# Spreading the 64-token output products of a fused attention and gated-MLP kernel over twelve slots, with their words made at slot heads

## The chip, the core and the metric

The kernel runs on one core of a Trainium2 chip. The metric is the device time of one execution in microseconds (us); lower is better. The engines are TensorE (PE, its weight loads are PEld), VectorE (DVE), ScalarE (ACT), GpSimd (POOL) and SyncE (SP), which issues most DMAs. Each engine takes its instructions in the order in which the program lists them for it.

## The reference

```python
def sm_attn(qq, kk, vv):              # softmax(scale * qq kk^T) vv, per batch and head
    ...
p_packed = sm_attn(p, k, v)           # 32 packing queries per head
x = sm_attn(q, p_packed, p_packed)    # (8 batches, 8 heads, 576 tokens, 64)
x = x.transpose(0, 2, 1, 3).reshape(4608, 512)
g, val = x @ w_gate, x @ w_val        # 512 -> 1536
out = (silu(g) * val) @ w_out         # 1536 -> 512, float32
```

## The kernel before

**Words.** Every float32 operand of a large product is split into a high word (a cast to fp32r, on ACT) and a low word (source minus high, on DVE, line 1194 in `low`). A product is then three matmuls: low by high, high by low, high by high.

**Batches and slots.** Batches 0 and 1 run first in other code. Batches 2 to 7 run in `batch2`, in twelve slots each, one for each chunk of 128 columns of the 1536 (`fc`, 0 to 11). A slot makes the gate and value products of one chunk (`gv_half`, line 1306): 12 matmuls of 256 columns for its first half, 12 of 320 columns for its second. ACT takes the SiLU (line 1315), DVE multiplies (`hmul2`, line 1324) into an h tile. Between these lie the calls of `fill`, which place the attention work of later batches by a table of slot and place (`run`), and in odd slots the 16 matmuls that make the next pair's weights (`m_part`, line 296).

**Output products.** For the 512 tokens of a batch that fill whole tiles of 128, `products` (line 1241) runs seven slots behind: 12 matmuls of 256 columns in the first half of a slot (`which` 0, on the words `ho`) and 9 in the second half (`which` 1, on `hs`). They add up over the six pairs of chunks of one half batch in four PSUM banks, `acc[0]` to `acc[3]`. Of `acc[1]` only the first 256 columns are used. At the sixth pair ACT and DVE take the banks out (`first_results`, `results`, line 1271).

**The 64-token products.** A batch has 576 tokens, so 64 are left over. Those of batches 2g and 2g+1 share one tile of 128 rows, `t4` (one small tile for each pair k of chunks), so there are four groups g of six pairs. `p4_step(k, b)` (line 1279) makes the words of pair k (one ACT cast, line 1285, one DVE subtraction, line 1194, both into `t_parts`, which holds two pairs; `t_first` in group 0) and at once issues the pair's six matmuls of 512 columns (`out_mm`, line 739). Where it is called sets what waits:

- group 0: in batch 2, slots 1 to 5, one pair a slot and two in slot 5. Batch 2 has no `products` before slot 7, so these slots are light.
- groups 1 and 2: all six pairs in one slot, slot 2 of batches 4 and 6 (`tail`), at the places 2 to 7 of `fill`.
- group 3: after the last slot, one pair in each of five rounds of the epilogue loop, between the two halves of `products`, and the sixth pair at the very end, through `end_out`, which also writes it out.

**PSUM.** Four banks hold `acc`. Four more are a ring that `gv_half`, `m_part` and the attention products take in turn (`ring_ps`); the sums of groups 1 to 3 take a ring bank too.

Of the kernel before, what the change touches and what calls it, by code (L numbers as in the profile page):

```python
# [25 lines left out]
P = 128  # L26
# [110 lines left out]
def tile_pack_attention_swiglu(ctx: ExitStack, tc: tile.TileContext, qT, q0, kT, v, vq, pT, wgv, wout, out):  # L137
# [547 lines left out]
    t4 = {}  # L685

    def t4_at(b, fc):
        k = fc // 2
        d = t4.setdefault(b // 2, {})
        if k not in d:  # L690
            d[k] = pool.tile([P, 2, P], F32, tag="t4", bufs=NFC // 2 + 1, name="t4")
        return d[k][:, fc % 2]
# [13 lines left out]
    def gv_chunk(b, fc, is_b, fill, behind, between):  # L706
        odd = b % 2
        n = NB if is_b else NA
        off = (0 if odd else 256) if is_b else (320 if odd else 0)
        mh, ml = ms[b, fc // 2]  # L710
        ah, al = a2[b]
        f = fc % 2
        pgs = []
        for s in range(2):
            pg = ring_ps("gv")
            pgs.append(pg)
            i = 0
# [11 lines left out]
        hf = early.tile([P, 256], F32, tag="hf", bufs=2, name="hf")  # L729
        o, o4 = (64, 0) if is_b and odd else (0, 256)  # L730
        nc.vector.tensor_tensor(hf, pgs[1][:, o : o + 256], sg[:, o : o + 256], op=ALU.mult)
        if is_b:
            r, r4 = slice(64 * odd, 64 * odd + 64), slice(o4, o4 + 64)
            nc.vector.tensor_tensor(t4_at(b, fc)[:, r], pgs[1][:, r4], sg[:, r4], op=ALU.mult)
        return h_split(hf, nc.scalar, nc.vector, between)
# [84 lines left out]
    with tc.manual_schedule(engines={mybir.EngineType.PE}):  # L820
        warm_ps = ps_aux.tile([P, 512], F32, tag="aux", name="warm_ps")

        ones = early.tile([P, 2 * P], F32, tag="hf", bufs=2, name="ones")
# [11 lines left out]
        with tc.manual_schedule(  # L835
# [135 lines left out]
            def half(i):  # L971
                fc, is_b = order[i]
                if fc // 2 < SPLIT:
                    return h0[fc // 2][:, fc % 2, 256 * is_b : 256 * is_b + 256]
                if i not in hs:
                    hs[i] = [early.tile([P, 256], F32, tag="hf", bufs=2, name="hf")]
                return hs[i][0]
# [7 lines left out]
            def hmul(i):  # L985
# [3 lines left out]
                if is_b:  # L989
                    r = slice(256, NB)  # L990
                    nc.vector.tensor_tensor(t4_at(0, fc)[:, :64], x[:, r], sg[:, r], op=ALU.mult)
# [5 lines left out]
            def h_low(i):  # L997
                hs[i].append(h_tile("hl"))
                nc.vector.tensor_tensor(hs[i][2], hs[i][0], hs[i][1].bitcast(F32), op=ALU.subtract)

# [82 lines left out]
        more = mid.tile([P, 4, 4 * P], F32, name="more")  # L1083
# [5 lines left out]

        def chunk(b, fc, is_b, fill, behind):  # L1090
            odd = b % 2
            n = NB if is_b else NA
            off = (0 if odd else 256) if is_b else (320 if odd else 0)
            mh, ml = ms[b, fc // 2]
            ah, al = a2[b]
            pgs = []
            for s in range(2):
                pg = ring_ps("gv")
                pgs.append(pg)
                todo = [(m_, a_, g) for m_, a_ in ((ml, ah), (mh, al), (mh, ah)) for g in range(NPAR)]  # L1100
                for i, (m_, a_, g) in enumerate(todo):
                    nc.tensor.matmul(
                        pg[:, :n], m_[:, g, fc % 2, s * P : (s + 1) * P], a_[:, g, off : off + n],
                        start=(i == 0), stop=(i == 5),
                    )
                fill()
            sg = pool.tile([P, NB], F32, tag="sg", bufs=1, name="sg")
            nc.scalar.activation(sg[:, :n], pgs[0][:, :n], AF.Silu)
            behind()
            at = b, int(is_b), fc // 2  # L1110
            if fc % 2 == 0:
                raw[at] = places.pop(0)
            x = raw[at][:, fc % 2].rearrange("p t n -> p (t n)")
            o, o4 = (64, 0) if is_b and odd else (0, 256)
            nc.vector.tensor_tensor(x, pgs[1][:, o : o + 256], sg[:, o : o + 256], op=ALU.mult)
            if is_b:
                r, r4 = slice(64 * odd, 64 * odd + 64), slice(o4, o4 + 64)
                nc.vector.tensor_tensor(t4_at(b, fc)[:, r], pgs[1][:, r4], sg[:, r4], op=ALU.mult)
# [106 lines left out]
        def products(at, which, fill):  # L1225
# [13 lines left out]
            for n, (bank, col, x, (wh, wl)) in enumerate(todo):  # L1239
                for i, (h_, w_) in enumerate(((lo, wh), (hi, wl), (hi, wh))):  # L1240
                    nc.tensor.matmul(  # L1241
                        acc[bank][:, QC * col : QC * col + QC], h_[:, x], w_,
                        start=(k == 0 and i == 0 and col == 0), stop=(k == 5 and i == 2 and (bank, col) in ((0, 1), (1, 0), (2, 1), (3, 1))),
                    )
                if n in ((1, 3) if which == 0 else (0, 2)):
                    fill()
            if k == 5:
# [12 lines left out]
        def results(b, half):  # L1260
# [16 lines left out]
        p4, t4_t = [], []  # L1277

        def p4_step(k, b):
            if k == 0:  # L1280
                t4_t.append(t4.pop(b // 2))
                p4.append(ps() if b > 1 else ps_acc.tile([P, 512], F32, tag="acc", name="acc4"))
            hh, hl = (t4_parts[:, k % 2, i] for i in range(2))
            src = t4_t[0].pop(k).rearrange("p f t -> p (f t)")
            nc.scalar.copy(hh, src)
            low(hl, src, hh)
            if k == 5 and b == B - 1:
                end_out(p4[0], (b // 2) * 2 * S + 4 * P, (hh, hl))
            else:
                for i in range(2):  # L1290
                    out_mm(p4[0], hh, hl, i * P, 2 * k + i)
            if k == 5:
                if b < B - 1:
                    emit_out(p4[0], (b // 2) * 2 * S + 4 * P, 0)
                p4.clear(), t4_t.clear()
# [22 lines left out]
        def hmul2(b, fc, is_b, pg, sg):  # L1318
# [6 lines left out]
            if is_b:  # L1325
                r, r4 = slice(64 * odd, 64 * odd + 64), slice(o4, o4 + 64)
                nc.vector.tensor_tensor(t4_at(b, fc)[:, r], pg[:, r4], sg[:, r4], op=ALU.mult)

        def batch2(b):
            nonlocal u_t, t4_parts  # L1330
            run = plan_of(b)
            for fc in range(NFC):
                t = (b - 2) * NFC + fc
                cur, nxt = pair_at(t), pair_at(t + 1)
                tail = b % 2 == 0 and fc == 2 and b > 2
                count, step = [0], [0]
# [7 lines left out]
                def fill():  # L1344
# [18 lines left out]
                    if b == 2 and (fc, c) in ((1, 3), (2, 3), (3, 3), (4, 3), (5, 3), (5, 7)):  # L1363
                        p4_step(fc - 1 + c // 7, 1)
# [12 lines left out]
                for is_b in (False, True):  # L1377
                    pg = gv_half(b, fc, is_b, 0)
# [3 lines left out]
                    run(fc, "b" if is_b else "a")  # L1382
                    hmul2(b, fc, is_b, pg, sg)
# [3 lines left out]
                    if is_b:  # L1387
                        run(fc, "hb")
                        if nxt and fc % 2:
# [10 lines left out]
        with tc.manual_schedule(  # L1400
            engines={mybir.EngineType.DVE, mybir.EngineType.Activation, mybir.EngineType.Pool}
        ):
            for b in range(2, B):
                batch2(b)
            for j in range(7):
# [52 lines left out]
```

## Time and profile before

| | |
|---|---|
| median of 3 runs | 744.02 us (742.9 to 746.06) |
| profiled execution: its own time | 745.82 us |
| its span, first to last instruction | 744.0 us |
| PE busy | 707.9 us (95%) |
| DVE busy | 496.5 us (67%) |
| ACT busy | 394.4 us (53%) |
| POOL busy | 173.5 us (23%) |
| mean granted TensorE clock, of full speed | 0.984 |

Times are from the span's start. A timeline row gives the start, the duration, the engine (a q behind it: its sequencer issues), the line, the operation, out<-in, the shape, and how many alike follow each other (x6); a bracket gives the idle time of the engine before it and what ended it. The duration of a matmul is its latency: matmuls overlap, and the rate is the distance between two starts. Where a row holds several, its duration runs from the first start to the last end.

### The profile page before, as it was taken

To read this page: it belongs to the slowest core of one execution; us is meant where nothing else is said; L and a number is where in the kernel's file an instruction comes from. 1 tells how busy PE (TensorE), PEld (TensorE's weight loads), DVE (VectorE), ACT (ScalarE), POOL (GpSimd) and SP (SyncE) were. 2 spreads that over 40 slices of the span, in tenths; PEclk is the share of its full clock that TensorE was granted. 3 is DMA by queue.
4 is the path that set the end of the run, shared out by engine and by line. 5 is a ranking of instruction groups with operands and counts; after the bars stand their busy time and mean duration, and the time that the engine had idled before them with its cause. 6 is when DMAs were issued, how large, how long until landed. Compare 5 with 4: busy or idle time off the path is not lost.

```text
span 744.0 us, 16252 instructions
## 1 busy us (share of the span) xinstructions
PE 707.9 (95%) x6503; PEld 621.6 (84%) x6503; DVE 496.5 (67%) x1093; ACT 394.4 (53%) x714; POOL 173.5 (23%) x349
## 2 busy tenths in 40 slices
PE   7999999999976999999989999999989999999986
PEld 5778788788856798999968989899877998989976
DVE  4986776668643687678754787778862787545453
ACT  3888456536633475636634467546652556343331
POOL 0000001223311433231311313223221232323241
PEclk9999999999998999999989999999999999999999
DMA  9999983021240532434242333452430324210001
GB/s 359 349 348 341 339 344 118 3 71 59 91 150 0 195 126 91 179 129 162 102 146 81 128 128 136 144 189 91 177 143 16 115 87 170 87 57 30 1 29 43
DMA packets 25435, 103.26 MB, mean 139 GB/s; under 512 B 6672, under 2 KB 7952, under 8 KB 16656
## 3 DMA queue, kind: packets, MB, share of 16 engines
q1 hardware_dynamic: 25072, 102.00, 37.1%
q8 instruction: 51, 0.84, 0.4%
q10 hardware_dynamic: 288, 0.23, 0.1%
q14 instruction: 24, 0.20, 0.1%
HBM read 86.44 MB, written 15.78 MB: 137 GB/s over the span
## 4 chain that ended last, share of the span: by engine, by line
PE 90%; DVE 5%; ACT 3%; issue 1%; ACTq 0%; DVEq 0%
PE gv L1306 30%; PE acc L1241 25%; PE acc L739 10%; PE aux L296 6%; PE gv L966 5%; PE aux L739 4%; PE gv L720 4%; PE gv_aux L296 1%; PE gv_aux L520 1%; PE gv_aux L436 1%; PE warm_ps L827 1%; ACT L458 1%; DVE ot L1271 1%; PE gv_aux L864 0%; DVE a L508 0%
## 5 line engine op out<-in xcount | busy, mean ns | idle before, releaser
L1315 ACT ACTIVATE sg<-gv 128x256 f32<-128x256 f32 (+1 forms) x144 | 59.2, 411 | 127.4 <-PE gv L1306 121.3
L1306 PE MATMUL gv<-a2h,ml 128*128 128x256 f32 (+1 forms) x576 | 123.6, 296 | 0.0
L1306 PE MATMUL gv<-a2l,mh 128*128 128x256 f32 (+1 forms) x576 | 123.0, 295 | 0.0
L1306 PE MATMUL gv<-a2h,mh 128*128 128x256 f32 (+1 forms) x576 | 122.4, 294 | 0.0
L1306 PEld LDWEIGHTS gv<-a2h,ml 128*128 128x128 f32 x576 | 92.3, 190 | 1.3
L1306 PEld LDWEIGHTS gv<-a2l,mh 128*128 128x128 f32 x576 | 93.3, 190 | 0.0
L1306 PEld LDWEIGHTS gv<-a2h,mh 128*128 128x128 f32 x576 | 92.4, 189 | 0.0
L1208 POOL TENSOR_TENSOR extra<-extra 128x128 f32<-128x128 f32 x108 | 49.6, 473 | 176.0 <-DVE ho L1194 131.4
L1208 POOL TENSOR_TENSOR more<-more 128x128 f32<-128x128 f32 x108 | 49.3, 471 | 161.4 <-DVE ho L1194 120.8
L619 DVE TENSOR_TENSOR ml<-aux,mh 128x512 fp32r<-128x512 f32 (+1 forms) x94 | 59.8, 678 | 13.1 <-ACT mh L677 13.0
L1241 PE MATMUL acc<-wo_h,ho 128*128 128x256 f32 x288 | 67.2, 296 | 0.2 <-DVE ho L1194 0.2
L1324 DVE TENSOR_TENSOR more<-gv,sg 128x256 f32<-128x256 f32 x72 | 30.3, 420 | 53.9 <-PE gv L1306 37.9
L677 ACT CAST mh<-aux 128x512 fp32r<-128x512 f32 (+1 forms) x94 | 50.0, 583 | 29.6 <-PE aux L296 28.5
L1241 PE MATMUL acc<-t_w,hs 128*128 128x256 f32 x432 | 64.0, 284 | 1.0 <-DVE hs L1194 1.0
L1241 PE MATMUL acc<-t_w,ho 128*128 128x256 f32 x432 | 63.0, 282 | 0.0
L1241 PEld LDWEIGHTS acc<-wo_h,ho 128*128 128x128 f32 x288 | 49.6, 190 | 15.9 <-issue 14.8
L1241 PEld LDWEIGHTS acc<-t_w,hs 128*128 128x128 f32 x432 | 59.6, 191 | 2.1 <-DVE hs L1194 1.2
L1324 DVE TENSOR_TENSOR extra<-gv,sg 128x256 f32<-128x256 f32 x72 | 30.2, 420 | 43.3 <-PE gv L1306 38.7
L1241 PEld LDWEIGHTS acc<-t_w,ho 128*128 128x128 f32 x432 | 56.5, 189 | 0.2
L739 PE MATMUL aux<-wo_h,t_parts 128*128 128x512 f32 (+2 forms) x76 | 29.7, 438 | 13.2 <-DVE t_parts L1194 13.2
L1241 PE MATMUL acc<-wo_l,ho 128*128 128x256 f32 x144 | 40.6, 282 | 0.0
L296 PE MATMUL aux<-w_s,ppt 64*32 64x512 f32 x576 | 39.3, 601 | 0.0
(222 smaller groups left out, 1509.2 us busy)
## 6 DMA issues: line engine op xcount, KB each, us to landing
w_s<-wd SPq DMA_DIRECT2D x36, 1024.0 KB, 5.1
st<-in_wgv SPq DMA_DIRECT2D x12, 1024.0 KB, 7.1
k_t<-in_kT SPq DMA_DIRECT2D x16, 576.0 KB, 5.2
out<-ot SPq DMA_DIRECT2D x35, 256.0 KB, 2.2
q_t<-in_qT SPq DMA_DIRECT2D x14, 576.0 KB, 6.7
v_t<-in_vq SPq DMA_DIRECT2D x6, 1280.0 KB, 7.7
st<-in_wout SPq DMA_DIRECT2D x6, 1024.0 KB, 7.0
wd<-w SPq DMA_DIRECT2D x6, 1024.0 KB, 11.5
```

The costliest lines, as they stand in the source:

```text
L296: nc.tensor.matmul(outs[par][32 * hp : 32 * hp + 32], lhs(r, hp), rhs(r, hp), start=True, stop=True)
L436: nc.tensor.matmul(pss[par][NP * j : NP * j + NP, i * SQ : (i + 1) * SQ], p_t[r, 2 * g + i, :], k_t[r, j // 2, 2 * g + i, j % 2 * SQ : j % ...
L619: pin(nc.vector.tensor_tensor(*x[1], op=ALU.subtract))
L677: nc.scalar.copy(m[0][at], src)
L720: nc.tensor.matmul(pg[:, :n], m_[:, g, f, s * P : (s + 1) * P], a_[:, g, off : off + n], start=(i == 0), stop=(i == 5),)
L739: nc.tensor.matmul(acc[:, at], h_[:, c : c + P], w_[fc // 2][:, fc % 2, at], start=((fc == 0 or first) and i == 0), stop=(fc == NFC - 1 an ...
L966: nc.tensor.matmul(held[i][s][:, :n], m_[:, g, f, s * P : (s + 1) * P], a_[:, g, off : off + n], start=(j == 0), stop=(j == len(todo) - 1),)
L1208: nc.gpsimd.tensor_tensor(x[:, to], x[:, a], x[:, b], op=ALU.subtract)
L1241: nc.tensor.matmul(acc[bank][:, QC * col : QC * col + QC], h_[:, x], w_, start=(k == 0 and i == 0 and col == 0), stop=(k == 5 and i == 2 a ...
L1306: nc.tensor.matmul(pg[:, :n], m_[:, g, fc % 2, s * P : (s + 1) * P], a_[:, g, off : off + n], start=(i == 0), stop=(i == 5),)
L1315: nc.scalar.activation(sg[:, :n], pg[:, :n], AF.Silu)
L1324: nc.vector.tensor_tensor(x, pg[:, o : o + 256], sg[:, o : o + 256], op=ALU.mult)
```

## The change

The 64-token products are cut and moved:

- groups 1 and 2: `side_products` issues the pair's products in halves of 256 output columns, at the end of the first half of `products`, in the twelve slots in which half 1 of an odd batch and then half 0 of the next batch have their output products (slots 1 to 11 of batches 4 and 6 and slot 0 of the batch behind). The sum goes into the free half of `acc[1]`. DVE copies that half out behind `results` (`side_out`), and SP writes it, 256 columns at a time.
- words: `p4_words` makes them apart from the products. In groups 1 and 2 it is called at the head of the slot, for each pair twice, once for each column half. In group 0 it is called at the head of the slot in whose middle the products stay (the sixth pair: at the head of slot 5's second half). In group 3 it runs one pair ahead of the products.
- the last slot of batch 7: `split_low`, the low word of the pair that the epilogue begins with, comes ahead of that slot's last `hmul2`.
- `t4` becomes one tile of 16 places; an even batch's 64 tokens have ten places, an odd batch's six, and `p4_words` reads the two of a pair as one strided operand. The h tiles of batches 0 and 1 and the ones of the warm-up become slices of `more` (three h tiles in place of two).

```diff
+    def t4_places(g, k):
+        return (6 * g + k) % 10, 10 + k
...
     def products(at, which, fill):
...
+            if which == 0:
+                side_products(at, acc[1])
...
     def results(b, half):
...
+            side_out((b, half, 5), acc[1])
...
-        def p4_step(k, b):
...
+        def p4_words(g, k):
+            hh, hl = (t4_parts[:, k % 2, i].rearrange("p (f b t) -> p b f t", f=2, b=2) for i in range(2))
+            e, o = t4_places(g, k)
+            src = t4[:, e :: o - e][:, :2]
+            nc.scalar.copy(hh, src)
+            low(hl, src, hh)
+            t4_w[g, k] = tuple(t4_parts[:, k % 2, i] for i in range(2))
...
+        def side_of(at):
+            b, half, k = at
+            g = (b + half) // 2 - 1
+            return (g, k, 1 - half) if (b + half) % 2 == 0 and 0 < g < B // 2 - 1 else None
...
+        def side_products(at, bank):
...
+            for i in range(2):
+                for j, (h_, w_) in enumerate(((h[1], wo_h), (h[0], wo_l), (h[0], wo_h))):
+                    nc.tensor.matmul(
+                        bank[:, QC:], h_[:, i * P : i * P + P], w_[k][:, i, c * QC : c * QC + QC],
...
+        def side_out(at, bank):
...
+            nc.vector.tensor_copy(u_t, bank[:, QC:])
+            row = g * 2 * S + 4 * P
+            nc.sync.dma_start(out[row : row + P, c * QC : c * QC + QC], u_t)
...
-                    if tail and 1 < c < 8:
-                        p4_step(step[0], b - 1)
-                        step[0] += 1
...
                 for is_b in (False, True):
+                    if b == 2 and (1 <= fc <= 5 and not is_b or fc == 5):
+                        p4_words(0, fc - 1 + is_b)
+                    if cur and side_of(cur) and not is_b:
+                        p4_words(*side_of(cur)[:2])
...
+                    if is_b and t == (B - 2) * NFC - 1:
+                        split_low(nxt)
                     hmul2(b, fc, is_b, pg, sg)
...
                 if 0 < j < 6:
-                    p4_step(j - 1, B - 1)
+                    p4_words(last, j)
+                    p4_products(last, j - 1)
                 products(cur, 1, lambda: None)
-            p4_step(5, B - 1)
+            p4_products(last, 5)
```

**PE, slot 2 of batch 4.** Before, the pairs of group 1 stand between the gate and value products and the output products:

```order
L1306 MATMUL gv<-a2h,mh 128x256 x2
L739 MATMUL aux<-wo_h,t_parts 128x512
L739 MATMUL aux<-wo_l,t_parts 128x512
L739 MATMUL aux<-wo_h,t_parts 128x512 x2
L739 MATMUL aux<-wo_l,t_parts 128x512
L739 MATMUL aux<-wo_h,t_parts 128x512
L1241 MATMUL acc<-wo_h,ho 128x256
```

The same slot in the changed kernel (its lines are numbered anew; 1314 is `gv_half`, 1214 `products`, 1291 `side_products`):

```order
L1214 MATMUL acc<-wo_h,ho 128x256
L1214 MATMUL acc<-t_w,ho 128x256 x6
L1291 MATMUL acc<-wo_h,t_parts 128x256
L1291 MATMUL acc<-wo_l,t_parts 128x256
L1291 MATMUL acc<-wo_h,t_parts 128x256 x2
L1291 MATMUL acc<-wo_l,t_parts 128x256
L1291 MATMUL acc<-wo_h,t_parts 128x256
L1314 MATMUL gv<-a2h,ml 128x320 x2
```

Six matmuls of 256 columns behind the output products took the place of six times six of 512 columns, the first of which stood ahead of them.

**ACT, batch 2, slot 3's second half and slot 4** (`y` and `t_w` are the factors of batch 3's softmax and combined output weights). Before:

```order
L1315 ACTIVATE sg<-gv 128x320
L488 ACT_TABLE_LOAD
L488 ACTIVATE y_2722<-y_2722 128x40
L646 CAST t_w<-b_t 128x1024
L1315 ACT_TABLE_LOAD
L1315 ACTIVATE sg<-gv 128x256
L1285 CAST t_first<-t_902 128x256
```

After:

```order
L1323 ACTIVATE sg<-gv 128x320
L488 ACT_TABLE_LOAD
L488 ACTIVATE y_2666<-y_2666 128x40
L646 CAST t_w<-b_t 128x1024
L1260 CAST t_first<-t_98 128x2x2x64
L1323 ACT_TABLE_LOAD
L1323 ACTIVATE sg<-gv 128x256
```

The cast of the word moved ahead of the second table load and of the SiLU, and stays behind the first table load and the cast of `t_w`.

**DVE, the end of the program.** Before:

```order
L1194 TENSOR_TENSOR hs<-extra,hs 128x384
L1258 TENSOR_TENSOR ot<-acc,extra 128x256
L1271 TENSOR_TENSOR extra<-acc,extra 128x256
L1271 TENSOR_TENSOR ot<-acc,extra 128x256
L1271 TENSOR_TENSOR ot<-ot 128x256
L1271 TENSOR_TENSOR ot<-acc,extra 128x256
L1271 TENSOR_TENSOR ot<-acc,ot 128x256 x2
L1194 TENSOR_TENSOR t_parts<-t_7908,t_parts 128x256
L753 COPY ot<-aux 128x192
```

After:

```order
L1167 TENSOR_TENSOR t_parts<-t_98,t_parts 128x2x2x64
L1167 TENSOR_TENSOR hs<-extra,hs 128x384
L1234 TENSOR_TENSOR ot<-acc,extra 128x256
L1247 TENSOR_TENSOR extra<-acc,extra 128x256
L1247 TENSOR_TENSOR ot<-acc,extra 128x256
L1247 TENSOR_TENSOR ot<-ot 128x256
L1247 TENSOR_TENSOR ot<-acc,extra 128x256
L1247 TENSOR_TENSOR ot<-acc,ot 128x256 x2
L756 COPY ot<-aux 128x192
```

The last low word, which PE's last products need, moved from behind the six operations of `results` to ahead of them.

## Rows read from the trace of the kernel before

**Rows 1.** The page, part 4: the chain that ended last, by engine.

```profile
PE 90%; DVE 5%; ACT 3%; issue 1%; ACTq 0%; DVEq 0%
```

**Rows 2.** Waits of PE: us in total, times, longest us.

```profile
PE aux L739 <- DVE t_parts L1194: 13.2, 6, 3.3
PE acc L739 <- DVE t_first L1194: 12.3, 5, 4.7
```

**Rows 3.** Timeline of PE and PEld: rates at full clock.

```profile
378.32 0.82 PEld L1241 LDWEIGHTS acc<-t_w,hs 128*128 128x128 f32 x6
378.46 0.89 PE L1241 MATMUL acc<-t_w,hs 128*128 128x256 f32 x6
379.19 0.28 PE L1241 MATMUL acc<-wo_h,hs 128*128 128x256 f32 x1
...
391.72 0.61 PE L739 MATMUL aux<-wo_h,t_parts 128*128 128x512 f32 x2
392.18 0.39 PE L739 MATMUL aux<-wo_l,t_parts 128*128 128x512 f32 x1
```

**Rows 4.** Timeline of PE: slot 2 of batches 4, 5, 6, first row and next slot's first.

```profile
379.55 0.40 PE L1306 MATMUL gv<-a2h,ml 128*128 128x256 f32 x2
...
400.95 0.40 PE L1306 MATMUL gv<-a2h,ml 128*128 128x256 f32 x2
...
474.23 0.40 PE L1306 MATMUL gv<-a2h,ml 128*128 128x256 f32 x2
...
479.87 0.40 PE L1306 MATMUL gv<-a2h,ml 128*128 128x256 f32 x2
...
553.10 0.40 PE L1306 MATMUL gv<-a2h,ml 128*128 128x256 f32 x2
...
573.18 0.40 PE L1306 MATMUL gv<-a2h,ml 128*128 128x256 f32 x2
```

**Rows 5.** One stretch: busy us of PE, PEld, DVE, ACT, POOL; PEclk; DMA share, GB/s.

```profile
384.00:391.00 7.00, 6.66 (x22) 5.63 (x23) 0.96 (x3) 0.41 (x1) 0.00 (x0) 0.56 0.01 2
```

**Rows 6.** Timeline of PE, DVE and ACT in batch 2, slots 2 to 4.

```profile
211.17 1.22 DVE L638 TENSOR_TENSOR b_t<-wo_h,wo_l 128x1024 f32<-128x1024 f32 x1
...
215.13 0.50 PE L739 MATMUL acc<-wo_h,t_first 128*128 128x512 f32 x1 [3.13 <-DVE t_first L1194]
...
219.93 0.40 PE L1306 MATMUL gv<-a2h,ml 128*128 128x256 f32 x2
...
227.54 1.28 ACT L488 ACT_TABLE_LOAD   x1
...
228.97 1.03 ACT L646 CAST t_w<-b_t 128x1024 fp32r<-128x1024 f32 x1
...
234.06 0.79 PE L739 MATMUL acc<-wo_h,t_first 128*128 128x512 f32 x1 [4.72 <-DVE t_first L1194]
...
239.97 0.40 PE L1306 MATMUL gv<-a2h,ml 128*128 128x256 f32 x2
```

**Rows 7.** Operations on tile t_parts: count, ns min/median/max, first and last start.

```profile
L1285 ACT CAST t_parts<-t x18: 397/402/409, 383.2 to 735.4; 128x256 fp32r<-128x256 f32 x18
L1194 DVE TENSOR_TENSOR t_parts<-t,t_parts x18: 413/418/425, 383.8 to 738.5; 128x256 fp32r<-128x256 f32 x18
```

**Rows 8.** Timeline, batch 4 slot 1: DVE's multiply, PE's scores for a later batch.

```profile
374.06 0.41 DVE L1324 TENSOR_TENSOR more<-gv,sg 128x256 f32<-128x256 f32 x1
374.14 1.10 PE L436 MATMUL gv_aux<-k_t,p_t 64*32 64x144 f32 x32
```

**Rows 9.** Timeline of PE and SP in the epilogue.

```profile
709.37 0.98 PE L1241 MATMUL acc<-t_w,hs 128*128 128x256 f32 x6 [1.00 <-DVE hs L1194]
...
714.37 0.79 PE L739 MATMUL aux<-wo_h,t_parts 128*128 128x512 f32 x1 [2.12 <-DVE t_parts L1194]
...
738.98 0.41 PE L739 MATMUL aux<-wo_h,t_parts 128*128 128x320 f32 x1 [2.48 <-DVE t_parts L1194]
...
741.18 0.33 SPq L757 DMA_DIRECT2D out<-ot  x1
```

More of the change, by code (lines that the diff above doesn't have):

```diff
@@ L683, in m_part @@
         m_high(b, k, fcs)
-    t4 = {}
-    def t4_at(b, fc):
[L688 to L692, printed above, removed]
+    t4 = pool.tile([P, 16, 2, P // 2], F32, tag="t4", bufs=1, name="t4")
+    more = mid.tile([P, 4, 4 * P], F32, name="more")
+    hfs = [more[:, i, : 2 * P] for i in range(3)]
+    def t4_places(g, k):
+        return (6 * g + k) % 10, 10 + k
+    def t4_at(b, fc):
+        return t4[:, t4_places(b // 2, fc // 2)[b % 2], fc % 2]
     def h_tile(t):
@@ L821, in tile_pack_attention_swiglu @@
         warm_ps = ps_aux.tile([P, 512], F32, tag="aux", name="warm_ps")
-        ones = early.tile([P, 2 * P], F32, tag="hf", bufs=2, name="ones")
+        ones = more[:, 3, : 2 * P]
         nc.vector.memset(ones, 1.0)
@@ L1088, in tile_pack_attention_swiglu @@
         places = as_places(more.rearrange("p i n -> p (i n)"), 4)
[L1090 to L1118, printed above, removed]
         def batch1(b, behind):
@@ L1242, in products @@
                         acc[bank][:, QC * col : QC * col + QC], h_[:, x], w_,
-                        start=(k == 0 and i == 0 and col == 0), stop=(k == 5 and i == 2 and (bank, col) in ((0, 1), (1, 0), (2, 1), (3, 1))),
+                        start=(k == 0 and i == 0 and col == 0),
+                        stop=(k == 5 and i == 2 and (bank, col) in ((0, 1), (2, 1), (3, 1)) + (((1, 0),) * (not side_of(at)))),
                     )
@@ L1285, in p4_step, with p4_products @@
             nc.scalar.copy(hh, src)
             low(hl, src, hh)
[L1287 to L1288 removed]
+            t4_w[g, k] = tuple(t4_parts[:, k % 2, i] for i in range(2))
+        def p4_products(g, k, at=slice(0, DM)):
+            if k == 0:
+                p4.append(ps() if g else ps_acc.tile([P, 512], F32, tag="acc", name="acc4"))
+            h = t4_w.pop((g, k))
+            row = g * 2 * S + 4 * P
+            if k == 5 and g == B // 2 - 1:
+                end_out(p4[0], row, h)
@@ new lines, in side_products @@
+        def side_products(at, bank):
+            side = side_of(at)
+            if not side:
+                return
+            g, k, c = side
+            h = t4_w.pop((g, k))
+            for i in range(2):
+                for j, (h_, w_) in enumerate(((h[1], wo_h), (h[0], wo_l), (h[0], wo_h))):
+                    nc.tensor.matmul(
+                        bank[:, QC:], h_[:, i * P : i * P + P], w_[k][:, i, c * QC : c * QC + QC],
+                        start=False, stop=(k == 5 and i == 1 and j == 2),
+                    )
@@ L1297, in gv_half @@
+        def side_out(at, bank):
+            side = side_of(at)
+            if not side:
+                return
+            g, _, c = side
+            nc.vector.tensor_copy(u_t, bank[:, QC:])
+            row = g * 2 * S + 4 * P
+            nc.sync.dma_start(out[row : row + P, c * QC : c * QC + QC], u_t)
         def gv_half(b, fc, is_b, s):
@@ L1334, in batch2 @@
                 cur, nxt = pair_at(t), pair_at(t + 1)
-                tail = b % 2 == 0 and fc == 2 and b > 2
-                count, step = [0], [0]
+                count = [0]
                 if b == 2 and fc == 3:
```

41 lines of the change are left out of this document (19 added, 22 removed).

## The prediction

> **What bounds the kernel now.** I read the chain that ended last first: 90% of it is PE [rows 1], so what counts is PE's stream, its work and its holes. Then the list of PE's waits: two lines hold nearly all of it, 13.2 us before the 64-token products on `t_parts` and 12.3 us before those on `t_first`, both until DVE has made a low word [rows 2]. Everywhere else in batches 2 to 7 PE runs without a hole, and a slot is as long as its matmuls. Then the rates: six matmuls of 256 columns start 0.73 us before the next, 0.12 us each, and two of 512 columns 0.46 us, 0.23 us each [rows 3]. So columns cost the same in both widths.
>
> The waits cost more than their length. From 384 to 391 us, right behind the longest wait (3.3 us [rows 2]), the granted clock is 0.56 of full speed [rows 5]: PE was idle, and then most of the stretch ran at 1.2 instead of 2.4 GHz. The best measure is therefore whole slots. Slot 2 of batch 4 takes 21.40 us (379.55 to 400.95), the same slot of batch 5, which has everything but the 64-token products, 5.64 us (474.23 to 479.87), and slot 2 of batch 6 takes 20.08 us (553.10 to 573.18) [rows 4].
>
> **The change, part by part.**
>
> *Groups 1 and 2.* Their 36 matmuls of 512 columns are worth 36 x 0.23 = 8.28 us in each of the two slots. What is left is waste: 21.40 - 5.64 - 8.28 = 7.48 us in batch 4 and 20.08 - 5.64 - 8.28 = 6.16 us in batch 6, 13.64 us together. Spread out, the words are made at the head of a slot and used only after 12 gate and value matmuls and 12 output products, 24 x 0.12 = 2.9 us later, while a word takes 0.40 us on ACT and 0.42 us on DVE [rows 7]. So PE should not wait for them. The products become 72 matmuls of 256 columns for each group, 72 x 0.12 = 8.64 us in place of 8.28: 0.7 us more for both. Gain: 12.9 us.
>
> What the move adds on other engines: each pair's words are made twice, so 12 more casts and 12 more subtractions in all, and in 24 slots one of each at the slot's head. In most of these slots DVE has room. Where it has none is a slot in which PE, right behind the gate and value products, takes a ring bank that DVE's multiply must first have read. Batch 4 slot 1 is such a place: DVE comes out of `results` straight into the multiply at 374.06, and the scores that start at 374.14 and take that bank last 1.10 us [rows 8], until the multiply is done. A low word ahead of that multiply (0.42 us [rows 7]) goes straight to PE. I count slot 1 of batches 4 and 6 (one word each), slot 1 of batch 5 (the copy of `side_out`, taken like a word) and slot 7 of batches 4 and 6 (copy and word): seven times 0.4, a loss of 2.8 us. Nothing at all if the multiply has slack that I do not see. The four extra output DMAs stand on SP's queue ahead of loads of `w_s`, half a microsecond each in waiting for DVE's copy; those loads are needed a slot or more later, so I count nothing, and at most the 0.4 us four times.
>
> The strided read of `t4` and the strided write of the word are not in the trace. The nearest rows are the present words of as many elements [rows 7]; I take their times. At double the time (0.8 us) the five tight slots would lose another 2.1 us. A gain has no reason.
>
> *Group 0.* It has 12.3 us of waits [rows 2] and two slow stretches behind the longer ones. From 215.13 to 219.93 and from 234.06 to 239.97 PE runs six products (6 x 0.23 = 1.38 us) and 12 matmuls of 320 columns (by columns 12 x 0.144 = 1.73 us), 3.11 us of work, in 4.80 and 5.91 us [rows 6]: 1.69 and 2.80 us lost to the clock. Together 16.8 us. The words move to slot heads, but not out of the queues of ACT and DVE, so something stays. The second word stands on DVE behind the sum `b_t`, 1.22 us [rows 6], while PE has only 12 short matmuls (1.4 us) since the multiply that stands ahead of it: I leave 1.2 us. The fourth stands on ACT behind a table load, a small exponential and the cast of `t_w`, 2.46 us from 227.54 to 230.00 [rows 6]; then it takes 0.40 and 0.42 us [rows 7], 3.3 us in all behind a SiLU, in which PE has about 1.6 us of matmuls (the rest of one half slot and 12 short ones): I leave 1.7 us. The first word delays a multiply that the scores wait for, 0.4 us. No hole is then as long as the two (3.13 and 4.72 us) behind which the clock fell. Gain: 16.8 - 3.3 = 13.5 us. Behind it batch 2's chain (scores, gather through DRAM, factors, transposes) must keep up with a PE that arrives up to 13 us sooner; nothing in that chain hangs on the 64-token products, and every operation in it gets its turn sooner as PE does.
>
> *Group 3 and the epilogue.* PE waits 1.00 us for the first `hs`, 2.12 us for the first word and 2.48 us for the last [rows 9]. `split_low` ahead of the multiply starts POOL's sums about a microsecond sooner, which takes away the first. The first word is made in the last slot, which takes away the second, with some 1.7 us of slow clock behind it (six products and as many matmuls at half speed). Then PE meets the chain ACT, DVE, POOL, ACT, DVE of the next pair, for which I leave 0.8 us. At the end the last word no longer waits behind `results`; but the copies do, so of the 2.7 us from the last low word (738.5 [rows 7]) to the DMA at 741.18 [rows 9] about 0.8 us stay, a copy and an addition, a gain of 1.9. Together 1.00 + 2.12 + 1.7 - 0.8 + 1.9 = 5.9 us.
>
> *Early part.* Three h tiles in place of two, in batches 0 and 1: DVE waits less for ACT, PE not at all on that. Nothing, within 0.3 us.
>
> **Sum.** 12.9 - 2.8 + 13.5 + 5.9 = 29.5 us. The profiled execution took 745.82 us (span 744.0 and 1.8 us around it), so it would take 716.3 us; the median of the runs, 744.02, lies 1.8 us lower, so 714.5 us.
>
> **Rivals.**
>
> *All waits go.* Without the 3.3 us left in group 0, the 2.8 us in the tight slots and the 0.8 us in the epilogue the gain is 36.4 us: 707.6 us. For it: each of these is an estimate at the edge of slack. Chance 0.09.
>
> *Group 0 keeps its long waits.* The second and the fourth word come as late as now, because the queue and not the place in the slot made them late: 3.13 + 1.69 + 4.72 + 2.80 = 12.3 us in place of the 2.9 us left, 723.9 us. For it: ACT's table load and cast still stand ahead [rows 6]. Against: the word no longer waits for the second table load, the SiLU and the multiply. Chance 0.07.
>
> *All 24 slots pay.* If every slot lost a word on both engines, 0.82 us, the loss is 19.7 us and not 2.8: 731.4 us. Against: in most slots the multiply is not what PE waits for next, and PE now has 0.7 us more work in each. Chance 0.05.
>
> *Weight loads come bare.* Halving the width doubles the weight loads, 36 more in each group. A load lasts about 0.19 us (six in 0.82 us, overlapping); were each added to PE's stream, 72 x 0.19 = 13.7 us: 728.2 us. Against: today's loads begin while the matmul before them runs, and 256 columns cost 0.12 us with a load for each [rows 3]. Chance 0.02. The Trainium skill, "TensorE: Matmul & The Clock Gate", section "The mechanism", says that a weight load overlaps with matmuls in flight only when it goes to another row group; all loads here take all 128 rows, so by it the loads would be bare, and by the page's 128 / 1.2 ns for a load (section "LDWEIGHTS (loading the stationary operand)") the cost is, as an estimate, 7.7 us and the time 722. The trace speaks against it [rows 3].
>
> *Slower.* The word at the slot head blocks ACT's SiLU and DVE's multiply behind it, PE runs out of ring banks for as long as it now waits in slot 2 of batches 4 and 6, and the clock falls behind each hole. One such slot costs 6.2 to 7.5 us, as there. Five of the 24 cancel the gain; from six on the kernel is slower, 714.5 + 6 x 6.2 = 751.7 us. Against: the words' sources are old by then, and slots without a 64-token product have no hole today. Chance 0.05, of which 0.02 end within 0.5%.
>
> **How the numbers follow.** The forecast has 0.72, with a range of its own of 709.5 to 720. With the rival above it that is 0.81, so the range is 707 to 721; the top takes in the doubled strided words (716.6) and a loss of half of the epilogue's gain besides. Faster by over 0.5% (3.7 us, about what a measurement of this kernel can tell from no change) are all cases but the last: 0.95; within 0.5%: 0.02; slower: 0.03.
>
> **What would show it.** In the changed profile: no wait for `t_parts` in batches 4 and 6, and their slots at 5.64 us plus 0.7; the wait for `t_first` near 3 us and the clock at 1.0 in batch 2; scores in slots 1 of batches 4 to 6 longer by 0.4 us; the time from PE's last `hs` products to the end shorter by 1.9 us. I am wrong where the clock stays low in batch 2, where a new wait on a ring bank shows in the twelve slots, or where POOL's chain, and not PE, sets the epilogue.

## Result and profile after

The changed kernel takes 716.15 us (median of 4 runs, 714.91 to 716.27), the kernel before 743.8 us beside it (median of 4, 742.9 to 746.06). The ratio is 0.962, 95% interval 0.9596 to 0.9644: 3.8% faster. Forecast were 714.5 us and a range of 707 to 721. The profiled execution took 716.15 us (its span is 714.4 us), 29.67 us less than the 745.82 us of before; the sum of the forecast was 29.5 us.

The page, its first and second part (busy time by engine; the span in 40 slices, granted clock in tenths), and the chain that ended last:

```profile
PE 698.5 (98%) x6575; PEld 616.5 (86%) x6575; DVE 503.9 (71%) x1107; ACT 397.9 (56%) x726; POOL 175.3 (25%) x349
...
PEclk9999999999999999999999999999999999999999
...
PE 85%; DVE 7%; ACT 4%; issue 2%; DMA 2%; DVEq 0%; ACTq 0%
```

PE is busy 98% of the span in place of 95%. Its busy time fell by 9.4 us although its work grew: in the slow stretches matmuls had lasted longer. The list of PE's waits (us in total, times, longest us) has nothing left on `t_parts`, and 2.6 us on `t_first` in place of 12.3 [rows 2]:

```profile
PE acc L742 <- DVE t_first L1167: 2.6, 2, 1.8
PE gv_aux L520 <- DVE a L508: 1.3, 2, 0.9
PE gv_aux L436 <- DVE more L1332: 0.9, 3, 0.3
```

In the changed kernel `gv_half` is line 1314, `products` 1214, `side_products` 1291, `out_mm` 742, `low` 1167, the cast of a word 1260, `hmul2` 1332. Timeline of PE, batch 4, first rows of slots 2 and 3, and the six new matmuls of slot 2:

```profile
368.32 0.40 PE L1314 MATMUL gv<-a2h,ml 128*128 128x256 f32 x2
...
371.12 0.28 PE L1291 MATMUL acc<-wo_h,t_parts 128*128 128x256 f32 x1
371.23 0.28 PE L1291 MATMUL acc<-wo_l,t_parts 128*128 128x256 f32 x1
371.35 0.40 PE L1291 MATMUL acc<-wo_h,t_parts 128*128 128x256 f32 x2
371.59 0.28 PE L1291 MATMUL acc<-wo_l,t_parts 128*128 128x256 f32 x1
371.71 0.28 PE L1291 MATMUL acc<-wo_h,t_parts 128*128 128x256 f32 x1
...
374.68 0.40 PE L1314 MATMUL gv<-a2h,ml 128*128 128x256 f32 x2
```

The slot that took 21.40 us [rows 4] takes 6.36 us, that is 5.64 + 0.72: six matmuls at 0.12 us, each with its own weight load, and no wait. By the rule that the prediction quoted from the Trainium skill ("TensorE: Matmul & The Clock Gate", section "The mechanism") the loads would have been bare. These rows disagree, as [rows 3] did. The same section also lets a load into a background weight buffer run ahead; whether that is what happens here, no run shows.

From batch 2 on, the stretches of the two profiled executions add up as follows. "Rest" is from batch 2's first slot to the end; starts of slots are those of their first matmul.

| us | start of batch 2 | batch 2 | batch 3 | batches 4 to 7 up to the last slot | last slot and epilogue | rest |
|---|---|---|---|---|---|---|
| before | 196.71 | 90.55 | 78.89 | 334.49 | 43.39 | 547.32 |
| after | 197.71 | 77.28 | 78.89 | 323.55 | 36.94 | 516.66 |
| gain | -1.00 | 13.27 | 0.00 | 10.94 | 6.45 | 30.66 |

### The profile page after: what moved, and what is told of

Same layout as the page of the kernel before. It is cut to its first block, busy times and chain, and to the rows that moved or that the text cites. A ratio compares the mean times of both kernels' runs of the same rounds, so it can differ in the third digit from the quotient of the medians.

```text
span 714.4 us, 16428 instructions
## 1 busy us (share of the span) xinstructions
PE 698.5 (98%) x6575; PEld 616.5 (86%) x6575; DVE 503.9 (71%) x1107; ACT 397.9 (56%) x726; POOL 175.3 (25%) x349
## 4 chain that ended last, share of the span: by engine, by line
PE 85%; DVE 7%; ACT 4%; issue 2%; DMA 2%; DVEq 0%; ACTq 0%
PE gv L1314 30%; PE acc L1214 26%; PE acc L742 9%; PE aux L296 5%; PE gv L721 4%; PE gv L969 3%; PE acc L1291 2%; DVE ot L1247 1%; PE gv_aux L296 1%; PE gv_aux L520 1%; DMA st<-in_wgv 1%; PE gv_aux L436 1%; PE aux L742 1%; PE warm_ps L830 1%; ACT top L222 1%
## 5 line engine op out<-in xcount | busy, mean ns | idle before, releaser
L742 PE MATMUL acc<-wo_h,hl 128*128 128x512 f32 x96 | 39.2, 408 | 0.0
```

The costliest lines, as they stand in the source:

```text
L742: nc.tensor.matmul(acc[:, at], h_[:, c : c + P], w_[fc // 2][:, fc % 2, at], start=((fc == 0 or first) and i == 0), stop=(fc == NFC - 1 an ...
```

## Experiments

My theory: the gain is the sum of three separate ones, each of them PE's waits on words and the slow clock behind them. The rivals: spreading the products is what gained; or the places of the words matter little, and other edits (h tiles, `t4`) freed the engines. The kernel before moved between 743.8 and 746.1 us from one set of runs to the next, so times are compared as ratios to it, and stretches through the column "rest" of the traces.

**Epilogue undone.**

```diff
-            p4_words(last, 0)
...
-                    p4_words(last, j)
+                    p4_words(last, j - 1)
                     p4_products(last, j - 1)
...
+            p4_words(last, 5)
             p4_products(last, 5)
```

and `split_low` behind the last multiply again.

> The changed kernel with only its epilogue undone: the words of group 3 are made right ahead of the products again, and the last split_low stands behind the multiply again. My theory (the gain is a sum of three separate ones, each a wait on words with the slow clock behind it; the epilogue's is 6.45 us by the two traces): 716.15 + 6.45 = 722.6 us, PE waits of about 1.0, 2.1 and 2.5 us on hs and t_parts back in the epilogue. Rival (the epilogue gained only because PE arrives there with other engines less behind, thanks to the spread products in the slots before): 716 to 718 us.

Ratio 0.9702 (0.9672 to 0.9733). The last stretch takes 44.16 us in place of 36.94, with the same waits on PE as in [rows 9]; two of the three:

```profile
685.49 0.98 PE L1214 MATMUL acc<-t_w,hs 128*128 128x256 f32 x6 [1.00 <-DVE hs L1167]
...
690.50 0.50 PE L742 MATMUL aux<-wo_h,t_parts 128*128 128x512 f32 x1 [2.14 <-DVE t_parts L1167]
```

The rival falls: all other stretches are as in the changed kernel (batch 2 77.33, batches 4 to 7 323.54 us). The 7.22 us are 0.77 more than the two traces gave, because the last hole was dearer this time: the granted clock from 711 us to the end is 0.74 here, and 1.00 from 735 us to the end in the kernel before. From PE's restart to the end it takes 5.80 us here (715.11 to 720.91) and 5.05 there (738.98 to 744.03).

**Only `split_low` undone.** The `split_low` edit by itself.

> The changed kernel with split_low behind the last multiply again, its epilogue words still one pair ahead. My theory (of the epilogue's 6.45 us that edit is worth the 1.00 us wait on the first hs): a wait of about 1 us on hs at the start of the epilogue returns and the time from the last slot's start to the end grows by 1.0 us. Rival (PE meets POOL's chain a round later anyway, so nothing is gained there): no difference in that stretch, less than 0.3 us.

Ratio 0.962 (0.959 to 0.965), too small a thing for the times, but the last stretch grew from 36.94 to 38.22 us, 1.28 us, and a wait of 1.05 us on `hs` is back. So of the epilogue `split_low` is 1.28 us and the words are the rest.

**Group 0 undone.**

```diff
+                        p4_words(0, fc - 1 + c // 7)
                         p4_products(0, fc - 1 + c // 7)
...
-                    if b == 2 and (1 <= fc <= 5 and not is_b or fc == 5):
-                        p4_words(0, fc - 1 + is_b)
```

> The changed kernel with only group 0 undone: its words are made in the middle of slots 1 to 5 of batch 2 again, right ahead of the products. My theory: five waits of about 2 to 4.7 us on t_first return, and the slow clock behind the longer ones, 13.25 us in all: 716.15 + 13.25 = 729.4 us. Rival (the waits there come from the softmax chain of batch 3 on DVE and ACT whatever the place of the words, and other edits such as the h tiles or the layout of t4 freed those engines): 716 to 720 us.

Ratio 0.9772 (0.9744 to 0.98). Batch 2 takes 90.40 us in place of 77.28: 13.1 us, near the 13.25 expected. The waits of [rows 6] are back, and the slow clock behind the longest; timeline of PE, and two stretches (busy us of PE, PEld, DVE, ACT, POOL; PEclk; DMA share, GB/s):

```profile
215.28 0.50 PE L742 MATMUL acc<-wo_h,t_first 128*128 128x512 f32 x1 [2.60 <-DVE t_first L1167]
...
234.20 0.80 PE L742 MATMUL acc<-wo_h,t_first 128*128 128x512 f32 x1 [4.76 <-DVE t_first L1167]
```

```profile
224.00:232.00 8.00, 4.79 (x30) 4.33 (x30) 3.64 (x14) 4.86 (x8) 1.78 (x3) 1.00 0.00 0
232.00:240.00 8.00, 5.80 (x18) 5.22 (x19) 2.11 (x4) 0.57 (x2) 1.54 (x2) 0.60 0.00 0
```

So the place of the words does it, with the h tiles and the layout of `t4` as in the changed kernel.

**One slot, words one place ahead.** Is it the spreading or the words? Groups 1 and 2 are back in slot 2 of batches 4 and 6, 512 columns wide, with words and products one place of `fill` apart; `side_products` and `side_out` are gone.

```diff
+                    if b in (4, 6) and fc == 2:
+                        if c < 7:
+                            p4_words(b // 2 - 1, c - 1)
+                        if c > 1 and c < 8:
+                            p4_products(b // 2 - 1, c - 2)
```

> The changed kernel with groups 1 and 2 back in slot 2 of batches 4 and 6, six matmuls of 512 columns a pair in a ring bank, but each pair's words made one place of fill ahead of its products. My theory (what was waste was the wait on words, so making them one pair ahead is enough; the spreading itself costs 0.7 us for narrower matmuls and 2.2 us in tight slots): 716.15 - 2.9 = 713.3 us, at most 715 with short waits, slot 2 of batches 4 and 6 at 5.64 + 8.28 = 13.9 us. Rival (six pairs in one slot are too much for ACT and DVE even when ordered one pair ahead, so spreading is what gained): waits on t_parts of a microsecond and more return and with them most of the 10.9 us, 722 to 727 us.

Ratio 0.9606 (0.958 to 0.9633). Batches 4 to 7 take 323.55 us, to the hundredth what the spread kernel takes. Slot 2 of batch 4 takes 15.31 us; it would be 13.92 without a wait (5.64 + 8.28), and one listed wait is left:

```profile
368.66 0.40 PE L1311 MATMUL gv<-a2h,ml 128*128 128x256 f32 x2
...
373.37 0.49 PE L742 MATMUL aux<-wo_h,t_parts 128*128 128x512 f32 x1 [0.86 <-DVE t_parts L1167]
...
383.97 0.40 PE L1311 MATMUL gv<-a2h,ml 128*128 128x256 f32 x2
```

So spreading by itself gained nothing: words made ahead are enough. I had expected 2.9 us less than the changed kernel here; the holes in the two slots, 1.4 us each, took them back.

**Spread, words late.** The other half of the question: the products stay spread, but the words are made right ahead of them.

```diff
             if which == 0:
+                if side_of(at):
+                    p4_words(*side_of(at)[:2])
                 side_products(at, acc[1])
...
-                    if cur and side_of(cur) and not is_b:
-                        p4_words(*side_of(cur)[:2])
```

> The changed kernel with the words of groups 1 and 2 made not at the slot's head but right ahead of their products, that is behind the multiply and behind the hs words on ACT and DVE; the products stay spread over twelve slots. My theory (the words must be ahead in the queues): behind the multiply (0.41 us) come the hs cast and low word (0.51 and 0.7 to 1.0 us) and then the t_parts cast and low word (0.40 and 0.42 us), about 2.4 us, against 1.44 us of output products on PE; some 0.5 to 1.0 us of waiting in each of those of the 24 slots that have no attention work on PE in between, 6 to 20 us in all: 722 to 736 us. Rival (spreading alone hides the words): 714 to 716.5 us, without the 2.2 us of the tight slots at best.

Ratio 1.0316 (1.0287 to 1.0346): slower than the kernel before. All 24 slots wait. The list of PE's waits, one slot of batch 4 on PE, DVE and ACT, and a stretch of it:

```profile
PE acc L1293 <- DVE t_parts L1167: 36.3, 24, 2.6
```

```profile
400.21 0.42 ACT L1262 CAST t_parts<-t 128x256 fp32r<-128x256 f32 x1
...
401.08 2.05 DVE L537 STREAM_TRANSPOSE ppt<-gv_aux 32x64 f32<-32x64 f32 x8
...
403.16 0.42 DVE L1167 TENSOR_TENSOR t_parts<-t,t_parts 128x256 fp32r<-128x256 f32 x1
...
403.64 0.39 PE L1293 MATMUL acc<-wo_h,t_parts 128*128 128x256 f32 x1 [1.59 <-DVE t_parts L1167]
```

```profile
419.00:431.00 12.00, 8.96 (x58) 8.55 (x57) 7.36 (x16) 5.91 (x9) 2.36 (x4) 0.86 0.30 101
```

Direction and cause are the theory's, the size is not: I had counted only the `hs` words ahead in the queues and 6 to 20 us. The attention work's own operations stand there too (here eight transposes, 2.05 us, between the cast and the low word), so slots with attention work, which I took for safe, wait as well. Batches 4 to 7 grew by 50.3 us, 14 more than the waits; part of the stretches behind them has a clock of 0.83 to 0.86.

**All words behind the multiply.** This and the next kernel ask where the rest of the tight slots' loss comes from (slot 1 of batch 4 takes 8.79 us and slot 7 8.97, where before 7.76 and 7.59 stood and 0.72 are the new matmuls).

```diff
-                    if cur and side_of(cur) and not is_b:
-                        p4_words(*side_of(cur)[:2])
...
                     hmul2(b, fc, is_b, pg, sg)
+                    if cur and side_of(cur) and not is_b:
+                        p4_words(*side_of(cur)[:2])
```

> The changed kernel with the words of groups 1 and 2 made directly behind the first half's multiply (ahead of the hs words) and not at the slot's head. My theory (the tight slots, slot 1 and 7 of batches 4 and 6, lose 0.3 to 0.7 us each beyond their six matmuls because a low word stands ahead of the multiply that PE's next ring bank waits for; behind the multiply it has 0.42 us of work against 1.44 us of output products on PE): slot 1 of batch 4 falls from 8.79 to about 8.5 us, slot 7 from 8.97 to about 8.3, 2 us in all, about 0.3% less time than the changed kernel, and no new wait on t_parts over 0.3 us. Rival (those slots are longer for another reason, such as the copy of side_out or results, and a word behind the multiply waits like the one behind the hs words): the slots stay, and waits on t_parts of 0.3 to 1 us come in slots without attention work on PE, up to 1% slower than the changed kernel.

Each was right in part. Slots 1 and 7 of batch 4 fell to 8.46 and 8.61 us, with batch 6 1.4 us in all in place of 2. But nine waits on `t_parts`, 7.3 us, came in even slots (slot 2 of batch 4: 7.79 in place of 6.36), and the ratio is 0.971 (0.9684 to 0.9736). ACT in slot 2, with the word now behind a table load and an exponential of the attention work:

```profile
368.90 1.28 ACT L458 ACT_TABLE_LOAD   x1
370.20 0.68 ACT L458 ACTIVATE e<-e 128x576 f32<-128x576 f32 x1
370.79 0.39 ACT L1260 CAST t_parts<-t 128x256 fp32r<-128x256 f32 x1
```

In the changed kernel, with the word at the slot's head, the cast runs at 366.90 us, 2.8 us ahead of the same load (369.67 us there).

**Behind the multiply in odd slots only.** The same move with `and fc % 2 == 0` at the head and `and fc % 2` behind the multiply.

> The changed kernel with the words of groups 1 and 2 behind the first half's multiply in odd slots only, and at the slot's head in even slots. My theory now (where the words stand matters twice: at the head they delay the multiply in slots 1 and 7, which have a matmul stage on a ring bank right behind it; behind the multiply they come too late in even slots, where ACT's table load or a late SiLU stands ahead and PE has only 1.44 us of output products): slots 1 and 7 of batches 4 and 6 as in the run with all words behind (8.46 and 8.61 us), even slots as in the changed kernel (6.36 us), no wait on t_parts: 1.4 us less than the changed kernel's batches 4 to 7. Rival (the waits in even slots came from the odd slots' words, which then stand late in the queues): waits on t_parts of 0.5 us and more stay in even slots, batches 4 to 7 no shorter than in the changed kernel.

Slots 1 and 7 take 8.47 and 8.64 us, even slots 6.36, nothing waits on `t_parts`; batches 4 to 7 take 322.27 us, 1.28 less than in the changed kernel. Ratio 0.9595 (0.9573 to 0.9616), not to be told from 0.962; but in the five kernels with the changed kernel's code in batches 4 to 7 these take 323.51 to 323.60 us, so the 1.28 us are no chance. DVE and PE in batch 4 slot 1, first the changed kernel, then this one:

```profile
361.80 0.41 DVE L1167 TENSOR_TENSOR t_parts<-t,t_parts 128x256 fp32r<-128x256 f32 x1
362.13 0.41 DVE L1332 TENSOR_TENSOR more<-gv,sg 128x256 f32<-128x256 f32 x1
...
362.60 0.72 PE L436 MATMUL gv_aux<-k_t,p_t 64*32 64x144 f32 x30 [0.32 <-DVE more L1332]
```

```profile
360.69 0.41 DVE L1332 TENSOR_TENSOR more<-gv,sg 128x256 f32<-128x256 f32 x1
360.77 1.10 PE L436 MATMUL gv_aux<-k_t,p_t 64*32 64x144 f32 x32
361.02 0.41 DVE L1167 TENSOR_TENSOR t_parts<-t,t_parts 128x256 fp32r<-128x256 f32 x1
```

PE's scores wait 0.32 us for the multiply where the word stands ahead of it, and take 1.45 us from their first start (361.87) to their last end. Where it stands behind, no wait is listed and they take 1.10 us, as in [rows 8]. What is left in slot 7 (8.64 - 7.59 - 0.72 = 0.33 us) I put on the copy of `side_out`, which still stands ahead of the multiply; that was not tried.

**Group 0 half a slot earlier.** Words right behind a SiLU:

```diff
                     sg = silu2(is_b, pg)
+                    if b == 2 and (fc == 1 and not is_b or fc <= 4 and fc > 0 and is_b):
+                        p4_words(0, fc - 1 + is_b)
+                    if b == 2 and fc == 5 and not is_b:
+                        p4_words(0, 5)
```

> The changed kernel with the words of group 0 made half a slot earlier, right behind a SiLU and so in the shadow of the value product: the second word ahead of the sum b_t on DVE, the fourth ahead of the table load and the cast of t_w on ACT. My theory (what is left of group 0's waits, 2.6 us on t_first, comes from these two operations that stand ahead in the queues): both waits go, slots 2 and 4 of batch 2 shrink by some 0.8 and 1.8 us and the time by 0.3 to 0.4%. Rival (the softmax chain of batch 3 runs so late now that PE only meets another wait, on a or on the scores' bank, a few microseconds later): slots 2 to 5 of batch 2 keep their sum of about 28 us, no difference.

Ratio 0.9593 (0.9565 to 0.9622), not to be told from 0.962. Slots 2 and 4 of batch 2 fell from 5.60 and 6.64 to 4.52 and 4.97 us, slots 3 and 5 rose from 5.73 and 9.99 to 7.05 and 10.64: of 2.75 us 0.8 are kept. The theory named the right queue places, since the waits on `t_first` fell to 0.15 us, and the rival got the account, since PE arrived sooner at other work. In slot 3 that is `m_part`, whose ring bank the multiply frees only behind a SiLU (213.74 us) held up by a table load (212.45 us): its third matmul starts 1.27 us behind its first. The moved word has a share in that: on DVE its low word, whose cast stands behind that SiLU, and a reduction come ahead of the multiply (how much they cost was not tried). In slot 5 it is the attention products. DVE and PE:

```profile
214.50 0.43 DVE L1167 TENSOR_TENSOR t_first<-t,t_first 128x256 fp32r<-128x256 f32 x1 [2.45 <-ACT t_first L1260]
214.85 0.75 DVE L463 TENSOR_REDUCE z<-e 128x4 f32<-128x576 f32 x1
...
214.93 1.04 PE L296 MATMUL aux<-w_s,ppt 64*32 64x512 f32 x2
...
215.51 0.41 DVE L1332 TENSOR_TENSOR more<-gv,sg 128x256 f32<-128x256 f32 x1
...
216.20 1.09 PE L296 MATMUL aux<-w_s,ppt 64*32 64x512 f32 x14 [0.23 <-DVE t L1335]
...
222.20 0.50 PE L742 MATMUL acc<-wo_h,t_first 128*128 128x512 f32 x1 [0.15 <-DVE t_first L1167]
...
230.22 1.31 PE L520 MATMUL gv_aux<-v_t,a 128*32 128x64 f32 x76 [1.26 <-DVE a L508]
```

**Both ideas together.** Group 0 as just now, groups 1 and 2 in one slot, the first two pairs' words in the slot before.

```diff
+                    if b in (4, 6):
+                        if (fc, c) in ((1, 7), (1, 8), (2, 3), (2, 4), (2, 5), (2, 6)):
+                            p4_words(b // 2 - 1, c - 7 if fc == 1 else c - 1)
+                        if fc == 2 and 1 < c < 8:
+                            p4_products(b // 2 - 1, c - 2)
```

> Group 0 as in the run before, and groups 1 and 2 in one slot with words ahead, the first two pairs' words made in the slot before, so that all twelve words stand ahead of the ACT table load that held up the second one (wait 0.86 us and some short ones). My theory (waits on words are all that is left): slot 2 of batches 4 and 6 from 15.3 to 14.0 us, group 0 as in the run before; against the changed kernel 2.2 us for the tight slots, 0.7 us for the narrow matmuls and 2.5 us in group 0, some 5 us or 0.7% less: a ratio to the kernel before near 0.955. Rival (words made earlier block a multiply in the slot before by as much as they save): no difference from the changed kernel, 0.962.

712.05 us, ratio 0.9557 (0.9532 to 0.9583), the fastest of all. Slot 2 of batch 4 is 13.98 us (PE's first row of slots 2 and 3), 0.06 above the 13.92 of bare work:

```profile
365.83 0.40 PE L1311 MATMUL gv<-a2h,ml 128*128 128x256 f32 x2
...
379.81 0.40 PE L1311 MATMUL gv<-a2h,ml 128*128 128x256 f32 x2
```

The rest takes 513.12 us against 516.66 in the changed kernel: 2.66 us in batches 4 to 7, 0.71 in batch 2, 0.14 at the end. That is 3.5 us in place of the 5 expected: groups 1 and 2 gave 2.66 in place of 2.9, group 0 only 0.71 in place of 2.5, for the reason seen in the run before.

## Why the prediction was right

**Groups 1 and 2: 12.9 - 2.8 = 10.1 us forecast, 10.94 measured.** The waste of 13.64 us went as a whole, and the narrow products cost 0.72 us a slot, as forecast. The tight slots lost 2.14 us in place of 2.8: 0.31 and 0.35 in the two slots 1, 0.15 in slot 1 of batch 5, 0.66 and 0.67 in the two slots 7. They were the right five places. A word costs 0.31 to 0.35 us there in place of 0.4. The forecast did not see the other side of that place: behind the multiply the word costs more (all words behind it, 7.3 us of waits). The strided operands cost nothing in 23 of 36 low words (0.39 to 0.46 us, against 0.41 to 0.43 in [rows 7]); the other 13 are in the last section.

**Group 0: 13.5 us forecast, 13.23 measured** over slots 1 to 5, and 13.1 by undoing it. Left were 1.2, 1.7 and 0.4 us by the forecast. In the trace PE waits at the places named: 0.77 us for the second word, behind `b_t`, and 1.85 us for the fourth, behind the table load and `t_w`. Slot 1 takes 6.95 us, 0.56 more than the 7.83 of before without the wait of 1.44 us there, and in it the scores wait 0.24 us for the multiply. Of the 1.85 us the low word itself makes 0.74, not the 0.42 of the forecast: it started while an operation of POOL ran (last section). Timeline of ACT, POOL, DVE and PE at the fourth:

```profile
221.65 1.28 ACT L488 ACT_TABLE_LOAD   x1
222.94 0.24 ACT L488 ACTIVATE y<-y 128x40 f32<-128x40 f32 x1
223.09 1.03 ACT L646 CAST t_w<-b_t 128x1024 fp32r<-128x1024 f32 x1
224.03 0.40 ACT L1260 CAST t_first<-t 128x256 fp32r<-128x256 f32 x1
...
224.20 0.73 POOL L648 TENSOR_TENSOR t_w<-b_t,t_w 128x256 fp32r<-128x256 f32 x1 [8.32 <-ACT t_w L646]
...
224.46 0.74 DVE L1167 TENSOR_TENSOR t_first<-t,t_first 128x256 fp32r<-128x256 f32 x1 [1.76 <-ACT t_first L1260]
...
225.26 0.50 PE L742 MATMUL acc<-wo_h,t_first 128*128 128x512 f32 x1 [1.85 <-DVE t_first L1167]
```

The Trainium skill ("ScalarE: Activation LUTs", section "What ACT_TABLE_LOAD costs") gives a load 1283 ns and a drain of about 1380 ns besides. The load agrees; of the drain nothing is seen, as the load starts 0.02 us behind the SiLU ahead of it (which ends at 221.63) and the exponential 1.29 us after the load did.

**Epilogue: 5.9 us forecast, 6.45 measured.** `split_low` brought 1.28 in place of 1.00. From PE's last `hs` product to the end it was 7.81 us before (736.22 to 744.03) and is 6.49 (707.88 to 714.37): 1.32 us in place of 1.9, because `results` and the copies still follow each other on DVE. The first word brought the rest, 6.45 - 1.28 - 1.32 = 3.85 us in place of 2.12 + 1.7 - 0.8 = 3.0: the 0.8 us left for POOL's chain was not needed, and the longest distance between two matmuls there is 0.38 us.

**Early part: nothing within 0.3 us forecast, a loss of 1.00 us measured.** This is the term that was wrong in its bound, though hardly in its value. Ten kernels with the same code up to there (the changed one and all nine of the experiments) begin batch 2 between 195.85 and 197.72 us, the kernel before at 196.71, inside that spread. No effect of the h tiles is shown, and a bound narrower than the spread should not have been given.

**Sum.** -1.00 + 13.27 + 10.94 + 6.45 = 29.66 us. The two terms sized too low (0.8 and 0.6 us) stand against the early part and group 0; that the sum is nearer than its parts is luck. The last step, 1.8 us from the profiled execution to the median, did not come: the profiled execution of the changed kernel (716.15 us, forecast 716.3) lies at the median of its runs, and that of the kernel before 2 us above its own. So the median is 1.65 us above the 714.5 forecast, and between the medians the gain is 27.65 us.

**The rivals.** That all waits go did not come: the 2.6 us on `t_first` and the 2.14 us in tight slots are left. That every slot pays 0.82 us did not come: the even slots lie at 5.64 + 0.72. Nor did the mechanism of the slower case, a word at the slot's head that blocks the SiLU and the multiply: such a word cost 0.31 to 0.35 us, in four slots. A kernel with the products spread over the same slots can still be slower than before, but by the opposite order: with the words right ahead of their products it lost 50.3 us over 24 slots, 2.1 us each and not 6.2. It was the place at the slot's head, not the spreading, that kept this away.

## What to carry to other kernels

When an engine waits on a small product of other engines, look at the place of that product's instructions in the queues before moving the consumer: one place earlier was worth all that spreading the consumer over twelve slots was. Each place has a price on both sides, here a multiply held up by 0.3 us at the head of a slot, or a table load of 1.28 us ahead of the word behind the multiply; read for each candidate place what stands ahead on each queue and who waits behind. Measure holes in whole stretches, since the slow clock behind them can add to what they cost: with the late words 36.3 us of waits came with 50.3 us of lost time.

## What the hardware showed beside

**The same hole, two prices.** Seven kernels, the changed one among them, have the same group 0, with the same wait of 1.8 us before the fourth pair. In four of them the clock stays at 1.00 behind it and batch 2 takes 77.3 us; in three it falls, and batch 2 takes 78.7 us. Two stretches behind that wait, the changed kernel and then the one-slot kernel:

```profile
226.00:230.00 4.00, 4.00 (x28) 3.72 (x27) 3.86 (x10) 1.21 (x4) 1.19 (x2) 1.00 0.00 0
```

```profile
226.00:230.00 4.00, 4.00 (x18) 3.83 (x17) 3.01 (x7) 0.92 (x3) 1.25 (x2) 0.61 0.00 0
```

A clock of 0.61 means that most of that stretch ran at 1.2 GHz and not 2.4, and it costs 1.4 us. The prediction argued that no hole was left in group 0 as long as those of 3.13 and 4.72 us behind which the clock had fallen; a hole of 1.8 us was enough in three of seven executions. The trace of before could have warned of it: behind the hole of 2.12 us in the epilogue [rows 9], for which the prediction itself counted a slow clock, the granted clock is 0.58 from 714 to 716.5 us. The changed kernel's trace fell on the cheap side: with the slow clock its group 0 would have gained some 11.8 us (an estimate, 13.23 - 1.4). What decides between the two was not tried.

**Low words that last longer.** Of the 36 low words of the changed kernel 13 take 0.59 to 0.87 us in place of 0.42. Whenever a word starts while an operation of POOL runs that has more than 0.3 us left, it is one of the 13, and it ends some 0.28 us after that operation; all others start ahead of POOL's operation, near its end (up to 0.17 us left), or with POOL idle. One of the 13, with POOL's row beside it (three operations of 0.46 to 0.52 us):

```profile
382.74 1.49 POOL L1181 TENSOR_TENSOR extra<-extra 128x128 f32<-128x128 f32 x3 [7.53 <-DVE ho L1167]
382.81 0.68 DVE L1167 TENSOR_TENSOR t_parts<-t,t_parts 128x256 fp32r<-128x256 f32 x1 [0.21 <-ACT t_parts L1260]
```

The Trainium skill ("SBUF — State Buffer", section "SBUF: two separate sides") says that a DVE operation with two inputs in SBUF and a GpSimd operation that reads SBUF take one pair of ports in turn, whoever starts first for the whole instruction. All 36 starts in this trace agree with it; no run took POOL's work away to test it. The strided operands are not the cause: in the kernel before, whose words are contiguous, the one word of 24 that starts so, the second of group 0, takes 0.99 us (POOL and DVE; POOL's row is that of the operation running then):

```profile
214.07 0.72 POOL L641 TENSOR_TENSOR b_t<-b_t 128x256 f32<-128x256 f32 x1
214.09 0.99 DVE L1194 TENSOR_TENSOR t_first<-t,t_first 128x256 fp32r<-128x256 f32 x1 [0.71 <-ACT t_first L1285]
```

It ends the 3.13 us wait of [rows 6]. In the changed kernel none of the 13 lies in a tight slot, but three are words of group 0: the first (0.83 us) stands ahead of the multiply that the scores wait for, and the fourth (0.74 us) lengthens PE's longest wait by 0.32 us. The price of a word in the prediction, 0.42 us, is that of a word with POOL out of the way.
